# First batch in 512-token blocks with 128-token rows, weight products in tick 2, output copies that scale

## Chip, cores, metric

One core of a Trainium2 chip (trn2) runs the whole program as one launch. The metric is device time in microseconds (us). The kernel before takes 2289.72 us, the median of 3 runs (2289.04 to 2291.06).

## What is computed

x has 4 batches of 12480 tokens with 128 channels. 32 inducing points attend to all tokens of a batch, then every token attends to the 32 results, and a layer with a rational activation follows.

```python
def mab(q, kv):
    s = scale * (q @ kv.transpose(0, 2, 1))
    s = s - s.max(-1, keepdims=True)
    a = np.exp(s)
    a /= a.sum(-1, keepdims=True) + 1e-09
    return a @ kv
h = mab(I, x)                      # 32 rows per batch
x = mab(x, h).reshape(B * S, D)    # 49920 tokens
h = x @ w_in                       # 128 -> 2048
P = a[0] + a[1] * h + a[2] * h2 + a[3] * h3
Q = 1.0 + np.abs(b[0]) * np.abs(h) + np.abs(b[1]) * h2
out = (P / (Q + 1e-6)) @ w_out     # 2048 -> 128
```

The weights arrive as 64-bit words and are turned into 32-bit floats in the kernel (`convert_weights`, line 37: for each word VectorE, DVE in the profile, does six operations and GpSimd, POOL, one add between them).

## The kernel before

All engine calls pass one helper (line 187), so that nearly every row of the profile reads L187, and rows are told apart by their tile names. Within an engine the instructions run in the order in which the program issues them.

**First batch** (`before`, line 1062). `pass1(0)` multiplies the 32 inducing rows with the columns of x (input `x_c`, channels on the partitions): blocks of 480 tokens, four blocks to a group (tile `pc`), 7 groups. DVE copies each group into `e` and keeps a running maximum (`mxs`), from which `nmc` comes. ACT takes the exponentials of `e`. `pooled(0)` turns `e` on TensorE (PE) into `eT` by way of `pt`, 120 tokens to a chunk, and sums the rows of x (input `x_t`, 120 tokens on the partitions) weighted with it, in `ph`; DVE adds each group to `acc`. The fold of `acc` (`pq`), `H` and `HT` end it. Columns and rows of x lie in 9 rooms of the wide tile `row`, 1920 columns wide; a row load has 12 chunks and is issued as two DMAs, of 96 and of 24 partitions (`wide_rows`, line 390). Between these steps the steps of `converted` (line 331) are filled in on DVE; in group 3 DVE also sums `e`.

**Start of the main part** (`main`, line 1120). `pass3(0)` for group 0 makes the token weights `at` of the first four blocks. Pieces 0 and 1 make half of the stationary tile `st` (w_in times `HT`: `pg`, `gs`, `st`). Then ACT scales all of `w_out` by `z_rho`.

**Ticks** (`fast_ticks`, line 953). There are 832 units: 4 batches, 26 blocks of 480 tokens, 8 pairs of slices of the hidden layer. Each tick begins one unit: PE makes `hp` (`first`) and adds a constant to it (`by`, `same`), DVE masks or ACT takes the absolute value into a room of `row`, DVE makes `l`; ACT works on groups of ten units, with logarithm then sigmoid over wide rows of up to 3840 columns; DVE or POOL finishes `l`; 17 ticks behind, PE multiplies `l` with `w_out` into `po` (`second`), of which there is one buffer. After the last pair of a block two more matmuls with `lin` are added, and DVE copies `po` to `oT` (`fetch`, line 938), which goes to `out`.

**Side work** (`side`, line 847). In every tick a budget in us per engine (`SPARE`) lets two generators step on. `attend` (line 825) makes `at` for the blocks to come (tiles `pd`, `sT`, `ps`, `a`, `pa`, `hl`). `ahead` (line 797) first runs `products` and `linear(0)` and then the passes of the batches 1 to 3 (`xTa`, `pc`, `e`). `products` (line 600) makes two sums: `base` times all slices of w_out (32 small matmuls, all in `two`), and w_in, turned by PE into `pgt` and scaled by ACT into `wt`, times w_out, which gives `w_two`. `linear` (line 626) makes `lin` from `w_two` and `HT` (tiles `prep`, `gl`). `attend` isn't stepped before `linear(0)` is done. Where the ticks need what isn't ready, `until` (line 886) steps both generators with no budget until it is: in `second` for `made` (the end of `products`) and for "linear", in `first` for `at`. In this mode nothing of the main loop is issued between.

```python
for which in ("attend", "ahead") if not self.fast or "linear" in self.ready_cols[0] else ("ahead",):
...
if n % 2 == 0 and q == 0:
    self.until(lambda: key in self.at)
```

Of the kernel before, what the change touches and what calls it, by code (L numbers as in the profile page):

```python
# [10 lines left out]
F32 = mybir.dt.float32  # L11
# [6 lines left out]
ALU = mybir.AluOpType  # L18
# [184 lines left out]
class Kernel:  # L203
# [169 lines left out]
    def wide_columns(self, b):  # L373

        def load(g):
            n = min(4, self.NB - 4 * g) * BT
            t = self.room(f"xTw{b}_{g}")
            cuts = [0, BT, 2 * BT, n] if g == 0 and n > 2 * BT else [0, n]
            for lo, hi in zip(cuts, cuts[1:]):
                self.nc.sync.dma_start(out=t[:, lo:hi], in_=self.x_c[b, :, 4 * BT * g + lo:4 * BT * g + hi])  # L380
            return t

        ts = [load(g) for g in range(self.NG)]
        for g, t in enumerate(ts):
            for j in range(4):
                yield t[:, BT * j:BT * j + BT]
                if j == 0 and g > 0:
                    self.wide_rows(b)

    def wide_rows(self, b):  # L390

        xs = self.xs.setdefault(b, [])
        n = min(3 * HB, self.NCH - HB * len(xs))
        if n > 0:
            if len(xs) >= 2 * 3:
                self.words += [w for w in [next(self.loads, None)] if w]
            t = self.room(f"xw{b}_{len(xs)}")[0:TP, 0:n * C].rearrange("p (c d) -> p c d", d=C)
            for p in (slice(0, 96), slice(96, TP)):
                self.nc.sync.dma_start(out=t[p], in_=self.x_t[b, p, HB * len(xs):HB * len(xs) + n, :])
            xs += [t[:, HB * i:HB * i + HB] for i in range(n // HB)]  # L400

    def pass1(self, b):
# [6 lines left out]
        xs = Blocks([], self.wide_columns(b), ahead=False) if self.boot else self.cols.pop((b, "a"))  # L409
# [14 lines left out]
        if self.boot:  # L424
            self.wide_rows(b)
        else:
            self.xs[b] = [self.x_rows(b, n) for n in range(4)]
# [17 lines left out]
        self.e[b] = e  # L445
        self.exps.append(lambda: self.exp_rows(b, e, nmc))
        self.flush()

    def exp_rows(self, b, e, nmc):
# [8 lines left out]
        if g + n < self.NG:  # L458
            if self.boot:
                self.exp_rows(b, e, nmc)  # L460
            else:
                self.exps.append(lambda: self.exp_rows(b, e, nmc))
# [9 lines left out]
    def pooled(self, b, own=None):  # L472
# [17 lines left out]
        eTs, early, n = [], int(self.boot), C if self.boot else C + 1  # L490
# [3 lines left out]
        if early:  # L494
            yield from turned(0)
        for g in range(self.NG):
            nb = min(4, self.NB - 4 * g)
            if g + early < self.NG:
                yield from turned(g + early)
# [3 lines left out]
            for k in range(HB * nb):  # L503
# [5 lines left out]
                if c == 0 and self.boot and (4 * g + j) % 3 == 0 and g + j:  # L509
                    self.xs[b] = xs  # L510
                    self.wide_rows(b)
                nc.tensor.matmul(ph[M * c:M * c + M, 0:n], eT[:, c, M * j:M * j + M], xs[4 * g + j][:, c, :], start=(j == 0), stop=(j == nb - 1))
                if c == HB - 1 and not self.boot and 4 * g + j + 4 < self.NB:
# [7 lines left out]
            if early and g == self.NG // 2:
                full, rest = self.NB // 4, self.NB % 4
                nc.vector.tensor_reduce(out=acc[:, C:], in_=e[:, 0:full].rearrange("p g n -> p (g n)"), axis=mybir.AxisListType.X, op=ALU.add)
                if rest:
                    more, rows = ap.tile([P, 1], F32, tag="mx", name=f"sum{b}"), slice(0, M * rest)
                    nc.vector.tensor_reduce(out=more[rows], in_=e[rows, full], axis=mybir.AxisListType.X, op=ALU.add)
                    nc.vector.tensor_tensor(out=acc[rows, C:], in0=acc[rows, C:], in1=more[rows], op=ALU.add)
# [20 lines left out]
        self.HT[b] = HT  # L548

# [50 lines left out]
    def products(self):  # L600

        nc, ap, p = self.nc, self.ap, self.params
        two = self.ps_o.tile([P, 512], F32, tag="po", name="two")
        for f in range(self.NF):
            if f % 4 == 0:
                yield "pe", 1.0
            nc.tensor.matmul(two[:, C:2 * C], self.base, self.w_out[:, f], start=(f == 0), stop=(f == self.NF - 1))
        yield "v", 0.25
        nc.vector.tensor_scalar(out=self.base, in0=two[:, C:2 * C], scalar1=Z * Z / A16, scalar2=None, op0=ALU.mult)
        for j in range(self.NF // 4):  # L610
            yield "pe", 0.9
# [3 lines left out]
            wt = ap.tile([P, 512], F32, tag="gs", name=f"wt{j}", bufs=2)  # L615
            yield from self.act(lambda: nc.scalar.activation(wt, pt, AF.Identity, bias=0.0, scale=p.lin_scale))
            self.free()
            yield "pe", 1.0
            for i in range(4):
                f = 4 * j + i  # L620
                nc.tensor.matmul(two[:, 0:C], wt[:, P * i:P * i + P], self.w_out[:, f], start=(f == 0), stop=(f == self.NF - 1))
        yield "v", 0.25
        nc.vector.tensor_copy(out=self.w_two, in_=two[:, 0:C])
        self.made = True
# [291 lines left out]
    def second(self, u, ks=(0, 1)):  # L916
# [3 lines left out]
        if q == 0 and 0 in ks:  # L920
            self.until(lambda: self.made or not self.fast)
# [16 lines left out]
    def fetch(self):  # L938
# [5 lines left out]
        self.nc.vector.tensor_copy(out=oT, in_=po[:, 0:BT])  # L944
# [117 lines left out]
    def before(self):  # L1062
# [11 lines left out]
        ahead = self.pass1(0)  # L1074
        next(ahead)
# [7 lines left out]
        self.fill = self.converted(first)  # L1083
        for n, _ in enumerate(ahead):
            for _ in range(4 if n == 0 else 2 if n % 3 == 2 else 0):
                next(self.fill, None)
        self.fill = itertools.chain(self.fill, self.converted(self.words))
# [125 lines left out]
```

## Time and profile before

| what | value |
|---|---|
| median of 3 runs | 2289.72 us |
| the profiled execution: its time, its span | 2289.09 us, 2287.2 us |
| PE, DVE, ACT, POOL busy, share of the span | 94%, 94%, 92%, 65% |
| mean granted TensorE clock | 0.976 |
| DMA | 120.89 MB, mean 53 GB/s |
| chain that ended last | PE 40%, DVE 25%, issue 15%, ACT 14%, DMA 3% |

The busy shares are means over the span. In the 40 slices of 57 us that the page shows, PE, DVE and ACT are at 8 tenths or below in the first four and at 9 in nearly all others, so a stage of the start and the loop have to be read apart. The chain's steps that are named DMA lie in the first 200 us.

### The profile page before, as it was taken

To read this page: it belongs to the slowest core of one execution; us is meant where nothing else is said; L and a number is where in the kernel's file an instruction comes from. 1 tells how busy PE (TensorE), PEld (TensorE's weight loads), DVE (VectorE), ACT (ScalarE), POOL (GpSimd) and SP (SyncE) were. 2 spreads that over 40 slices of the span, in tenths; PEclk is the share of its full clock that TensorE was granted. 3 is DMA by queue.
4 is the path that set the end of the run, shared out by engine and by line. 5 is a ranking of instruction groups with operands and counts; after the bars stand their busy time and mean duration, and the time that the engine had idled before them with its cause. 6 is when DMAs were issued, how large, how long until landed. Compare 5 with 4: busy or idle time off the path is not lost.

```text
span 2287.2 us, 23816 instructions
## 1 busy us (share of the span) xinstructions
PE 2149.3 (94%) x7774; PEld 978.8 (43%) x7774; DVE 2145.6 (94%) x2363; ACT 2101.6 (92%) x1194; POOL 1481.9 (65%) x1030
## 2 busy tenths in 40 slices
PE   4688999999999999998999999989999999999998
PEld 2333444444444444443444444434444444444443
DVE  6786999999999999999999989999999999999995
ACT  1476999999999999998999999989999999999995
POOL 2144666767667666666666666766677776766667
PEclk7799999999999999999999999999999999999999
DMA  9214100220231112212221131001101001000000
GB/s 279 63 57 130 54 13 29 74 79 31 91 96 36 51 35 61 65 48 67 90 60 56 35 91 35 14 23 51 54 16 52 22 17 31 18 22 18 19 12 19
DMA packets 104540, 120.89 MB, mean 53 GB/s; under 512 B 13407, under 2 KB 101279, under 8 KB 104407
## 3 DMA queue, kind: packets, MB, share of 16 engines
q1 hardware_dynamic: 104406, 119.28, 17.5%
q8 instruction: 63, 1.03, 0.2%
q14 instruction: 71, 0.57, 0.1%
HBM read 80.89 MB, written 25.56 MB: 47 GB/s over the span
## 4 chain that ended last, share of the span: by engine, by line
PE 40%; DVE 25%; issue 15%; ACT 14%; DMA 3%; POOL 1%; SPq 1%; ACTq 0%; DVEq 0%; POOLq 0%
PE po L187 26%; DVE l L187 14%; ACT row L187 11%; PE hp L187 10%; DVE row L187 7%; ACT L187 2%; DMA row<-x_t 1%; PE ph L187 1%; PE pc L187 1%; DVE oT L187 1%; SPq L187 1%; POOL l L187 1%; PE pd L187 1%; DVE gl L187 1%; DMA raw<-w_out 1%
## 5 line engine op out<-in xcount | busy, mean ns | idle before, releaser
L187 PE MATMUL po<-l,w_out 128*128 128x480 f32 x3328 | 1555.3, 573 | 5.9 <-POOL l L187 3.3
L187 DVE SCALAR_TENSOR_TENSOR l<-row,all,hp 128x960 f32<-128x960 f32 x832 | 999.5, 1202 | 30.3 <-ACT row L187 24.0
L187 POOL TENSOR_TENSOR l<-row 128x960 f32<-128x960 f32 x416 | 931.4, 2239 | 34.6
L187 POOL TENSOR_SCALAR row<-l,all 128x960 f32<-128x960 f32 x416 | 445.2, 1070 | 672.1 <-DVE l L187 554.5
L187 PEld LDWEIGHTS po<-l,w_out 128*128 128x128 f32 x3328 | 617.6, 191 | 404.2 <-issue 239.9
L187 ACT ACTIVATE row<-row,all 128x3840 f32<-128x3840 f32 (+1 forms) x250 | 738.1, 2953 | 1.0
L187 ACT ACTIVATE row<-row 128x3840 f32<-128x3840 f32 (+1 forms) x250 | 715.8, 2863 | 9.4 <-DVE l L187 8.2
L187 DVE SCALAR_TENSOR_TENSOR l<-l,all,row 128x960 f32<-128x960 f32 x416 | 532.3, 1280 | 2.1 <-ACT row L187 2.1
L187 PE MATMUL hp<-at,st 128*128 128x480 f16 x1664 | 475.6, 368 | 41.5 <-DVE l L187 36.8
L187 ACT ACTIVATE row<-hp,all 128x960 f32<-128x960 f32 x416 | 436.4, 1049 | 51.8 <-PE hp L187 51.3
L187 DVE TENSOR_SCALAR row<-hp 128x960 int32<-128x960 int32 x416 | 475.1, 1142 | 9.3 <-PE hp L187 8.2
L187 PEld LDWEIGHTS <-st 128*128 128x128 f16 x1872 | 181.4, 97 | 523.1 <-issue 502.0
L187 PE MATMUL hp<-same,by 96*128 96x480 f16 x832 | 238.6, 367 | 23.5 <-DVE row L187 22.6
L187 ACT ACT_TABLE_LOAD x169 | 216.8, 1283 | 3.6 <-PEq L1206 0.7
L187 PEld LDWEIGHTS <-by 96*128 96x128 f16 x832 | 82.0, 99 | 215.6 <-issue 194.9
L187 DVE COPY oT<-po 128x480 f32<-128x480 f32 x104 | 67.6, 650 | 41.9 <-PE po L187 41.5
L187 PE MATMUL po<-at,st 128*128 128x480 f16 x208 | 60.5, 373 | 3.2 <-DVE st L187 3.2
L187 POOL TENSOR_TENSOR cv<-cv 128x384 f32<-128x384 f32 (+2 forms) x11 | 12.4, 1126 | 48.6 <-DVE cv L187 48.6
L187 POOL TENSOR_TENSOR a<-a,asm 120x512 f32<-120x512 f32 (+1 forms) x27 | 36.7, 1359 | 6.0 <-DVE asm L187 6.0
L187 DVE TENSOR_SCALAR_CACHE_REDUCE e<-pc 128x240 f32<-128x240 f32 (+1 forms) x56 | 20.5, 399 | 21.1 <-PE pc L187 21.1
L187 ACT ACTIVATE e<-e,nmc 128x960 f32<-128x960 f32 (+1 forms) x16 | 15.5, 986 | 26.4 <-DVE nmc L187 26.4
L187 ACT ACTIVATE hl<-pa 128x480 f16<-128x480 f32 (+1 forms) x28 | 15.6, 558 | 25.1 <-PE pa L187 23.3
(116 smaller groups left out, 610.7 us busy)
## 6 DMA issues: line engine op xcount, KB each, us to landing
xTb<-x_c SPq DMA_DIRECT2D x104, 240.0 KB, 2.8
out<-oT SPq DMA_DIRECT2D x104, 240.0 KB, 2.0
xTa<-x_c SPq DMA_DIRECT2D x78, 240.0 KB, 3.6
x<-x_t SPq DMA_DIRECT2D x78, 240.0 KB, 3.9
at<-hl SPq DMA_DIRECT2D x416, 30.0 KB, 1.8
row<-x_c SPq DMA_DIRECT2D x5, 960.0 KB
row<-x_t SPq DMA_DIRECT2D x8, 576.0 KB, 15.8
raw<-w_in SPq DMA_DIRECT2D x4, 480.0 KB
```

What stands on the lines that cost most here:

```text
L187: ins = call(*args, **kw)
```

## The change

1. `first_batch` takes the place of `pass1(0)` and `pooled(0)`: blocks of 512 tokens and chunks of 128. The columns come in nine tiles of 1536 (the last 192), the rows from a new input `x_r`, in which token 128k+p lies in partition p: one DMA of 128 partitions for each tile, into the room of the column tile that was read last. One load of w_out goes ahead of each row load. More steps of `converted` stand in the score groups: 4 and then 3 for each group.
2. `turned_weights` (the `pgt` turns and ACT's `wt`) stands between the pooled sums, from group 2 on; three `wt` lie in a room of `row`, the fourth in a `gs` buffer.
3. `sums`: POOL adds up the 16 slices of w_out, so that `base` is multiplied once. `products` and `linear(0)` are run whole in ticks 2 and 3, `checks` in tick 4; `ahead` begins with batch 1, `attend` is free from tick 4 on, and `made` with its wait is gone.
4. ACT no longer scales w_out; `fetch` multiplies by `z_rho` as it copies `po`.

```diff
-        xs = Blocks([], self.wide_columns(b), ahead=False) if self.boot else self.cols.pop((b, "a"))
+        xs = self.cols.pop((b, "a"))
...
+    def first_batch(self):
...
+        for lo in range(0, N, 3 * W):
+            cols.append(self.room(f"c{lo}"))
+            nc.sync.dma_start(out=cols[-1][:, 0:min(3 * W, N - lo)], in_=self.x_c[0, :, lo:min(lo + 3 * W, N)])
...
+            t = self.room(f"r{k}")[:, 0:12 * P].rearrange("p (k d) -> p k d", d=C)
+            nc.sync.dma_start(out=t[:, 0:n], in_=self.x_r[:, k:k + n])
...
+        self.some(4)
+        for g in range(groups):
...
+                nc.tensor.matmul(pc[M * j:M * j + M, 0:w], self.ind, cols[i // 3][:, lo:lo + w], start=True, stop=True)
+            self.some(3)
...
+            for _ in range(len(rows), len(cols) if g == groups - 1 else (blocks[-1] + 1) // 3):
+                self.words += [x for x in [next(self.loads, None)] if x]
+                load()
+        nmc = self.filled(self.largest(0, mxs), [1, 1])
...
+        ready = turned(0)
+        turns = self.turned_weights()
+        for g in range(groups):
+            eT, sizes = ready
+            if g + 1 < groups:
+                ready = turned(g + 1)
...
+                    nc.tensor.matmul(ph[M * c:M * c + M, 0:C], eT[0:d, c, M * j:M * j + M], rows[k // 12][0:d, k % 12], start=(j == 0), stop=(i == some[-1]))
+            self.some(5)
...
+            if g > 1:
+                next(turns, None)
...
+    def turned_weights(self):
...
+            lo = 2 * P + 4 * P * j
+            wt = self.row[:, self.rooms["u"] - 1, lo:lo + 4 * P] if j < 3 else self.ap.tile([P, 512], F32, tag="gs", name=f"wt{j}", bufs=2)
+            nc.scalar.activation(wt, pt, AF.Identity, bias=0.0, scale=p.lin_scale)
...
+    def sums(self):
...
+        G.tensor_tensor(out=part, in0=w[:, 0:n], in1=w[:, n:], op=ALU.add)
+        while n > 2 * P:
+            n //= 2
+            G.tensor_tensor(out=part[:, 0:n], in0=part[:, 0:n], in1=part[:, n:2 * n], op=ALU.add)
+        G.tensor_tensor(out=self.w_two, in0=part[:, 0:P], in1=part[:, P:2 * P], op=ALU.add)
...
+            nc.tensor.matmul(two[:, 0:C], wt, self.w_out[:, f], start=(f == 0), stop=(f == self.NF - 1))
+        nc.tensor.matmul(two[:, C:2 * C], self.base, self.w_two, start=True, stop=True)
...
-        if self.fast:
-            yield from self.products()
-            yield from self.linear(0)
...
-            self.until(lambda: self.made or not self.fast)
...
-        self.nc.vector.tensor_copy(out=oT, in_=po[:, 0:BT])
+        if self.fast:
+            self.nc.vector.tensor_scalar(out=oT, in0=po[:, 0:BT], scalar1=self.params.z_rho, scalar2=None, op0=ALU.mult)
...
-            p.checks()
-            nc.scalar.activation(self.w_out, self.w_out, AF.Identity, bias=0.0, scale=p.z_rho)
-        self.later = pieces[2:]
+            self.sums()
+        self.later = pieces[2:] + ([self.products(), self.linear(0), self.checked()] if fast else [])
...
+        "x_r": x[0, :N // P * P].reshape(N // P, P, C).transpose(1, 0, 2),
```

The instructions are moved in these places. `hp_0_2` is the `hp` of block 0, pair 2; the numbers at the end of a name count tiles.

SyncE's (SP's) queue of loads, first batch. Before, from the third load of rows on (`row<-x_t`; `raw` is a load of w_out):

```order
L187 DMA row<-x_t 96x1536
L187 DMA row<-x_t 24x1536
L187 DMA row<-x_t 96x1536
L187 DMA row<-x_t 24x1536
L187 DMA raw_236<-w_out 128x384
L187 DMA row<-x_t 96x1536
L187 DMA row<-x_t 24x1536
L187 DMA raw_250<-w_out 128x384
```

After, from the first load of columns on:

```order
L187 DMA row<-x_c 128x1536 x8
L187 DMA row<-x_c 128x192
L187 DMA raw_213<-w_out 128x384
L187 DMA row<-x_r 128x1536
L187 DMA raw_226<-w_out 128x384
L187 DMA row<-x_r 128x1536
L187 DMA raw_241<-w_out 128x384
L187 DMA row<-x_r 128x1536
```

A tile of rows is now one DMA of 128 partitions instead of two of 96 and 24, a load of w_out stands ahead of each from the first on, and each row load waits for the column tile whose room it takes.

DVE, the products and `linear(0)`. Before, between unit 22 (`l_2_6`) and the mask of unit 24 (`hp_3_0`):

```order
L187 SCALAR_TENSOR_TENSOR l_2_6_970<-row,all,hp_2_6_939 128x960
L187 COPY sT_1_991<-pd_1_978 128x480
L187 SCALAR_TENSOR_TENSOR gl_995<-prep_993,base 128x128
L187 TENSOR_REDUCE amx_1_683<-ps_1_997 120x16
L187 TENSOR_TENSOR a_1_682<-ps_1_997,amx_1_683 120x512
L187 SCALAR_TENSOR_TENSOR gl_995<-gl_995 128x128 x4
L187 SCALAR_TENSOR_TENSOR st_547<-gl_995 64x128 x3
L187 MEMSET st_547 64x64
L187 TENSOR_SCALAR row<-hp_3_0_962 128x960
```

After, between the masks of units 2 and 4 (`hp_0_2`, `hp_0_4`):

```order
L187 TENSOR_SCALAR row<-hp_0_2_677 128x960
L187 SCALAR_TENSOR_TENSOR l_0_1_694<-row,all,hp_0_1_664 128x960
L187 TENSOR_SCALAR base<-two 128x128
L187 COPY w_two<-two 128x128
L187 SCALAR_TENSOR_TENSOR l_0_2_722<-row,all,hp_0_2_677 128x960
L187 SCALAR_TENSOR_TENSOR gl_726<-prep_724,base 128x128
L187 SCALAR_TENSOR_TENSOR gl_726<-gl_726 128x128 x4
L187 SCALAR_TENSOR_TENSOR st_566<-gl_726 64x128 x3
L187 MEMSET st_566 64x64
L187 TENSOR_SCALAR row<-hp_0_4_718 128x960
L187 SCALAR_TENSOR_TENSOR l_0_3_740<-row,all,hp_0_3_690 128x960
```

The whole of `linear(0)`, from `gl` to the memset, stands 20 units earlier, ahead of the mask of unit 4; `sT`, `amx` and `a` of attend's group 1 are no longer beside it.

SP, the DMAs that spread `hl` of group 1 into `at_1_0` (needed by unit 32, `hp_4_0`). Before:

```order
L187 DMA xTa_18_1160<-x_c 128x480
L187 DMA xTa_19_1163<-x_c 128x480
L187 DMA xTa_20_1170<-x_c 128x480
L187 DMA xTa_21_1173<-x_c 128x480
L187 DMA xTa_22_1176<-x_c 128x480
L187 DMA xTa_23_1179<-x_c 128x480
L187 DMA at_1_0_1191<-hl_1_1188 32x480 x8
```

After:

```order
L187 DMA xTa_12_967<-x_c 128x480
L187 DMA xTa_13_970<-x_c 128x480
L187 DMA xTa_14_973<-x_c 128x480
L187 DMA xTa_15_976<-x_c 128x480
L187 DMA out<-oT_0_1056 128x480
L187 DMA at_1_0_1084<-hl_1_1042 32x480 x8
```

Before, the `at` DMAs are queued behind 24 column loads of batch 1 (`xTa`, the last six shown); after, behind 16 and the first output. DVE's last operation ahead of them, `hl_1`, is behind `l_3_1` (unit 25) after, and before it stood between `pc_4` and `pc_5` of batch 1 with only `l_2_0`, `l_3_6` and `pc_5` left to the mask of unit 32.

## Rows read from the trace of the kernel before

**Rows 1.** Windows by stage: window, length, PE PEld DVE ACT POOL busy (x), PEclk, DMA share, GB/s.

```profile
32.40:68.40 36.00, 18.86 (x237) 12.73 (x237) 22.01 (x45) 7.38 (x11) 6.00 (x6) 0.55 0.92 214
...
85.40:102.10 16.70, 12.31 (x68) 7.54 (x69) 13.48 (x14) 9.76 (x13) 5.15 (x6) 1.00 0.08 22
102.10:128.20 26.10, 17.99 (x76) 11.49 (x75) 20.07 (x19) 26.05 (x16) 5.25 (x4) 0.80 0.00 0
...
144.50:153.90 9.40, 4.21 (x20) 1.38 (x20) 6.64 (x15) 5.90 (x3) 0.44 (x1) 0.84 0.63 209
...
171.20:194.30 23.10, 14.16 (x46) 2.82 (x46) 6.96 (x22) 4.35 (x3) 3.03 (x4) 0.87 0.58 176
...
500.00:1400.00 900.00, 876.25 (x3280) 399.48 (x3279) 878.28 (x931) 869.11 (x491) 610.64 (x437) 0.99 0.20 60
```

**Rows 2.** Windows of two stretches of loading: columns, then rows with w_out.

```profile
12.00:24.00 12.00, 8.89 (x39) 0.97 (x36) 7.97 (x29) 0.00 (x0) 2.98 (x4) 0.74 1.01 425
26.00:42.00 16.00, 10.15 (x91) 6.29 (x87) 10.42 (x31) 5.21 (x7) 3.34 (x3) 0.61 1.03 220
```

**Rows 3.** Timeline of PE, 85 to 98 us: start, us, instruction, count, [idle before].

```profile
85.38 0.98 PE L187 MATMUL hp<-at,st 128*128 128x480 f16 x4 [1.91 <-POOL st L187]
...
94.46 1.95 PE L187 MATMUL two<-w_out,base 128*128 128x128 f32 x16
```

**Rows 4.** Timeline of ACT, 84 to 215 us.

```profile
87.63 2.00 ACT L187 ACTIVATE w_out<-w_out,all 128x2048 f32<-128x2048 f32 x1 [2.12 <-DVE w_out L187]
...
100.09 0.68 ACT L187 ACTIVATE wt<-pgt,all 128x512 f32<-128x512 f32 x1
...
102.08 3.40 ACT L187 ACTIVATE row<-row 128x3840 f32<-128x3840 f32 x1
...
128.24 3.40 ACT L187 ACTIVATE row<-row 128x3840 f32<-128x3840 f32 x1
...
210.62 3.40 ACT L187 ACTIVATE row<-row 128x3840 f32<-128x3840 f32 x1
```

**Rows 5.** Timeline of DVE at two copies of the output, blocks 1 and 13.

```profile
198.63 0.66 DVE L187 COPY oT<-po 128x480 f32<-128x480 f32 x1 [1.05 <-PE po L187]
...
446.01 0.65 DVE L187 COPY oT<-po 128x480 f32<-128x480 f32 x1
```

**Rows 6.** Timeline of DVE, 30 to 72 us.

```profile
32.22 0.15 DVE L187 COPY nmc<-pb 128x1 f32<-128x1 f32 x1
...
38.59 0.29 DVE L187 COPY acc<-ph 128x128 f32<-128x128 f32 x1 [3.12 <-PE ph L187]
...
46.26 1.15 DVE L187 TENSOR_SCALAR cv<-raw 128x384 int32<-128x384 int32 x1
47.45 0.56 DVE L187 SCALAR_TENSOR_TENSOR cv<-raw,cv 128x384 int32<-128x384 int32 x1
48.04 0.36 DVE L187 TENSOR_SCALAR cv<-cv 128x384 int32<-128x384 int32 x1
...
55.85 3.14 DVE L187 TENSOR_REDUCE acc<-e 128x1 f32<-128x2880 f32 x1
```

**Rows 7.** Chain of waits, 0 to 150 us: start, us, step.

```profile
22.13 15.98 DMA row<-x_t
```

**Rows 8.** Timeline of DVE, 143 to 156 us.

```profile
149.28 1.26 DVE L187 SCALAR_TENSOR_TENSOR gl<-gl 128x128 bf16<-128x128 f32 x4
```

**Rows 9.** Groups by form: names, shapes xcount | busy us, mean ns | idle before.

```profile
L187 POOL TENSOR_TENSOR l<-row 128x960 f32<-128x960 f32 x416 | 931.4, 2239 | 34.6
...
L187 DVE COPY oT<-po 128x480 f32<-128x480 f32 x104 | 67.6, 650 | 41.9 <-PE po L187 41.5
...
L187 DVE COPY HT<-HT 128x128 f32<-128x128 f32 x4 | 1.1, 281 | 0.2 <-PE HT L187 0.2
```

**Rows 10.** DMA issues, part 6 of the page: out<-in, count, KB each, us to landing.

```profile
at<-hl SPq DMA_DIRECT2D x416, 30.0 KB, 1.8
```

**Rows 11.** The tile gs: ns min/median/max, first and last start, form.

```profile
L187 DVE TENSOR_SCALAR gs<-pg,all x24: 466/500/535, 524.2 to 1486.2; 128x256 f32<-128x256 f32 x24
```

More of the change, by code (lines that the diff above doesn't have):

```diff
@@ L423, in pass1, with largest @@
             self.free()
[L424 to L427, printed above, removed]
+        self.xs[b] = [self.x_rows(b, n) for n in range(4)]
+        nmc = yield from self.largest(b, mxs)
+        self.e[b] = e
+        self.exps.append(lambda: self.exp_rows(b, e, nmc))
+        self.flush()
+    def largest(self, b, mxs):
+        nc, ap = self.nc, self.ap
+        X = mybir.AxisListType.X
         yield "v", 0.1
@@ L458, in exp_rows @@
         if g + n < self.NG:
[L459 to L462, printed above, removed]
+            self.exps.append(lambda: self.exp_rows(b, e, nmc))
     def flush(self):
@@ L508, in pooled @@
                     ph = self.misc(f"ph{b}_{g}")
[L509 to L513, printed above, removed]
+                nc.tensor.matmul(ph[M * c:M * c + M, 0:C + 1], eT[:, c, M * j:M * j + M], xs[4 * g + j][:, c, :], start=(j == 0), stop=(j == nb - 1))
+                if c == HB - 1 and 4 * g + j + 4 < self.NB:
                     xs.append(self.x_rows(b, 4 * g + j + 4))
@@ L516, in pooled, with rows_of @@
             if g == 0:
-                nc.vector.tensor_copy(out=acc[:, 0:n], in_=ph[:, 0:n])
+                nc.vector.tensor_copy(out=acc, in_=ph[:, 0:C + 1])
             else:
-                nc.vector.tensor_tensor(out=acc[:, 0:n], in0=ph[:, 0:n], in1=acc[:, 0:n], op=ALU.add)
+                nc.vector.tensor_tensor(out=acc, in0=ph[:, 0:C + 1], in1=acc, op=ALU.add)
             self.free()
[L521 to L527, printed above, removed]
+        yield from self.rows_of(b, acc)
+    def rows_of(self, b, acc, own=None):
+        nc, ap = self.nc, self.ap
         yield "pe", 0.3
@@ L598, in split @@
         self.ready_cols[b].add(which)
[L600 to L609, printed above, removed]
+    def turned_weights(self):
+        nc, p = self.nc, self.params
+        self.wt = []
         for j in range(self.NF // 4):
-            yield "pe", 0.9
             pt = self.misc(f"pgt{j}")
@@ L1082, in before @@
         nc.vector.memset(self.ceps, CEPS)
[L1083 to L1087, printed above, removed]
-        self.filled(self.pooled(0, self.cp.tile([C, 4 * M], F32, name="HT0")), [5] * self.NG + [2, 2])
+        self.fill = itertools.chain(self.converted(first), self.converted(self.words))
+        self.first_batch()
     def filled(self, gen, most):
         last = None
-        for need, _ in gen:
+        while True:
+            try:
+                need, _ = next(gen)
+            except StopIteration as done:
+                return done.value
             if need == "v" and last == "pe":
-                for _ in range(most.pop(0)):
-                    next(self.fill, None)
+                self.some(most.pop(0))
             last = need
```

142 lines of the change are left out of this document (94 added, 48 removed).

## The prediction

> **What bounds the kernel now.** I read the windows first, stage by stage, because the busy shares of the whole span hide the start. In the loop, from 500 to 1400 us, PE, DVE and ACT are busy 97%, 98% and 97% of the time [rows 1]: there nothing waits, and an edit is worth what it adds to or takes from all three at once. The stages before it look different. From 12 to 24 us the DMA engines are full (1.01) and bring 425 GB/s of columns, while DVE is busy 8.0 of 12 us [rows 2]. From 32.4 to 68.4 they are at 0.92, but move only 214 GB/s, while PE is busy 18.9 us of 36 and DVE 22.0 [rows 1]. From 144.5 to 153.9 and from 171.2 to 194.3 ACT is busy 5.9 of 9.4 and 4.4 of 23.1 us [rows 1]. These two gaps are `until`: side work that the ticks need is made up with the main loop standing still.
>
> Then the timelines, for the borders of the stages. The first `hp` starts at 85.38 [rows 3]. Of ACT's logarithms [rows 4] the first group starts at 102.08, the second at 128.24, and the fourth only at 210.62. Ten units lie between two groups, so that the last step is 82.4 us for twenty units. In undisturbed ticks with side work the output copies of blocks 1 and 13 stand at 198.63 and 446.01 [rows 5]: 247.4 / 12 = 20.6 us for a block of eight units, 25.8 for ten.
>
> The terms below are against the profiled execution, 2289.1 us, which is 0.6 under the median of the three runs; I add the 0.6 at the end.
>
> **(a) Pass 1: +2.0.** Twenty-four steps of the conversion stand ahead of the maximum instead of 17, so 7 more on DVE. At 384 wide a step takes 0.36 or 0.56 us [rows 6], at 480 by the same slope 0.45 to 0.7: 3 to 4 us, and a step behind POOL's add can wait. But DVE has a third of the time free while the columns come [rows 2], and these come no later. Ends: 0 (all hidden) and +4; I take the middle. So `nmc`, at 32.22 before [rows 6], comes at about 34.3.
>
> **(b) Pass 2: -8.6.** It lasts from 32.4 to 68.4 us because the rows are late: the chain stays on one row load for 15.98 us [rows 7]. The two stretches of loading, at equal DMA share [rows 2], show why: columns, 128 partitions a DMA, came at 425 GB/s, rows and w_out, the rows in DMAs of 96 and 24, at 220. After the change a row tile has 128 partitions of 6144 bytes in one DMA, the shape of the new column tiles, so I take 425: rows and w_out are 8.5 MB, 20 us, from the end of the columns (26.4) to about 46.5. Then DVE bounds the pass. The first `acc` comes 6.2 us after `nmc`, as before (38.59 against 32.4) [rows 6]. Behind it DVE has 14 SCALAR_TENSOR_TENSOR at 0.55, 15 TENSOR_SCALAR at 0.36, 7 sums of 0.29, the reduction of `e` at 3.14 x 3072/2880 with 0.5 beside it, and about 4 waits for POOL's add (a `cv` of the same size took 1.15 instead of 0.36, so 0.8 each) [rows 6], less some overlap at the starts: 21.2. In total 27.4 instead of 36.0. PE isn't later: its 18.9 us of now [rows 1] and some 4 for the 16 turns of w_in that come in are 23, all at the granted clock of this stage, 0.55, so mostly at the 1.2 GHz level. Ends: with rows at 220 GB/s as before the last lands at about 65, and (a) and (b) together bring 1.8 instead of 6.6; without any wait for POOL it is 3.2 better.
>
> **(c) From acc to HT: -0.6**, as fewer conversion steps are left to stand between. So (a) to (c) bring the first `hp` from 85.4 to about 78.2.
>
> **(d) Ticks 0 to 7: +4.1.** Here the products begin to cost. PE's product is in tick 2: 17 matmuls of two passes each, at 1.95/16 = 0.122 a pass [rows 3], 4.1 us. Before, 32 passes (3.9 us) lay in the same ticks, but nothing of DVE stood behind them; now the copies of `base` and `w_two` do, ahead of `l_0_2`, and of the 4.1 I take 0.6 as covered by the mask and `l_0_1` ahead: 3.5. Then `gl` with its thirds is ahead of the mask of unit 4: eight operations at 1.26/4 = 0.31 [rows 8] and a memset, 2.6. Gone from here is ACT's scaling of w_out, 2.00 us [rows 4], which held up its first absolute value. 3.5 + 2.6 - 2.0 = 4.1. `sums` on POOL, 1920 elements wide in all, takes 1920/960 x 2.24 [rows 9] = 4.5 us and is hidden: it starts before tick 0, and the product comes some 6 us later. If that cover went, the product would wait for it, which with `gl` operations held by POOL makes the upper end, +8.5; the lower is 0 (all of it beside ACT's work).
>
> **(e) Ticks 7 to 17: -0.5.** ACT is the bound here, 26.05 of 26.1 us busy [rows 1]. Three `wt` at 0.68 [rows 4] leave for pass 2, where ACT is busy 7.4 of 36 [rows 1]; the exponentials of group 1's `a` (some 0.6) come in. DVE then is nearly as full, hence not the whole 1.4.
>
> **(f) Ticks 17 to 37: -29.9.** All three uses of `until` lie here. `made` is gone; "linear" is done in tick 3; attend is free from tick 4 instead of tick 24, so that `hl_1` stands behind unit 25 and its DMAs are issued four ticks, some 10 us, ahead of `hp_4_0`. Each takes 1.8 us to land [rows 10]; only if none of the eight overlapped another (14 us) would they be late. So the 82.4 us become 2 x 25.8 = 51.5, -30.9; less 1.0, since by unit 37 `ahead` has made five of batch 1's score groups, where before it had six, and the loop has that to do later.
>
> **(g) The copies: +3.5.** 104 copies of 0.650 us [rows 9] become TENSOR_SCALAR with a pointer scalar, from PSUM. Before has no such row of 480 wide. The nearest is `gs`, the same operation with one or two pointer scalars at 256 wide: 0.466 at least, 0.500 in the middle, 0.535 at most [rows 11]. A copy of 256 would take 0.281 + 128 x (0.650 - 0.281)/352 = 0.415 [rows 9]. The scalars thus cost 0.05 to 0.12; I take 0.055, the end with one scalar. 104 x 0.055 = 5.7 us of DVE. The loop is full, and `po` has one buffer for which the next block waits, so it isn't hidden; but PE and ACT are equally long, so not all of it counts. Ends: 0 and 5.7.
>
> **Sum:** 2.0 - 8.6 - 0.6 + 4.1 - 0.5 - 29.9 + 3.5 = -30.0; 2289.1 - 30.0 + 0.6 = **2259.7 us**.
>
> **The rivals.** *R1, the gaps' work is paid back in the loop.* In the gaps DVE was busy 6.6 and 7.0 us [rows 1], of which some 8 is side work (the rest is a mask, a copy and three `l`), and the loop has no DVE time to spare. Paid in full it is 2268. Against: the 25.8 for ten units already holds ten ticks' side work. *R2, the rows come no faster.* Lines of 6144 bytes came at 220 GB/s; the pitch between partitions stays long, and that may be the cause and not the 96 + 24. Then 6.6 - 1.8 = 4.8 are lost: 2264. *R3, slower:* a DVE operation on `cv` took 1.15 instead of 0.36 beside POOL [rows 6]. If each scaled copy waits for POOL like that, 104 x 0.8 = 83 us come in: 2339. It decides from (30 + 3.5)/104 = 0.32 us a copy. Against: the 24 `gs` operations read PSUM beside a POOL that is busy two thirds of the loop [rows 1], and the longest took 0.535 [rows 11]. The Trainium skill, "SBUF — State Buffer", section "SBUF: two separate sides", has the port of DVE and POOL locked by certain DVE operations with sources in SBUF; the copy reads PSUM, so by it this doesn't happen, and `gs` agrees. *R4, a gap stays:* if pair 2's `at` lands late, or attend isn't in fact earlier, up to the 23.1 us of the second gap [rows 1] come back: 2282. The order above speaks against it. *R5, the scalar is free:* the copy's time is set by its 480 columns alone. Then (g) is nil: 2256.2. Against: the shortest `gs` is over the line of the copies by 0.05. The Trainium skill, "VectorE: DVE Perf Modes", section "The TRN2 errata — SBUF-src ops pay a fixed extra latency per instruction", speaks for it: an operation from PSUM costs 120 + N cycles at 0.96 GHz, by estimate 625 ns here (the row: 650), with no term for the scalar.
>
> **How the numbers follow.** The forecast gets 0.62, R1 0.12, R2 0.10, R5 0.10, R4 0.03, R3 0.03. The range: 2259.7 less the bounds 2.0 of (a), 3.2 of (b), 4.1 of (d) and 3.5 of (g) is 2247; 2259.7 plus 8 of R1 and 4.4 of (d) is 2272, which takes in R2 with the upper bounds of (a) and (g). R3 and R4 are left out. What a measurement of this kernel can tell from no change is 0.2%, 4.6 us; all cases but R3 end below that: faster 0.96, same 0.01, slower 0.03.
>
> **What would show it.** In the profile after: `nmc` near 34; DMA at or above 400 GB/s while rows load, and the last `acc` near 62; first `hp` near 78; the first logarithm some 21 us behind it; no stretch of ten us with ACT half idle between 80 and 200 us; logarithm groups 26 us apart; `oT` as TENSOR_SCALAR at 0.65 to 0.71. It is wrong if the row loads run at 220 GB/s (R2), if `xTa` and `pc` still stand in the chain ahead of `hp_4_0` (R4), if blocks 2 to 13 take more than 20.6 us each (R1, if by side work; (g), if by `oT`), or if `oT`'s longest is far over its median (R3).

## The result, and the profile after

The changed kernel takes 2258.44 us (median of 4 runs, 2257.45 to 2260.96), beside 2290.27 for the kernel before (4 runs): ratio 0.9863, 95% interval 0.9846 to 0.988. The profiled execution took 2257.45 us with a span of 2255.6, 31.6 less than before.

Windows of the changed kernel, by its own stage borders (columns as in [rows 1]); the last line is the stretch of row loads, which answers to the second of [rows 2]:

```profile
34.60:62.00 27.40, 15.14 (x239) 11.30 (x240) 22.29 (x46) 9.62 (x16) 6.11 (x6) 0.75 0.48 190
78.20:100.50 22.30, 16.56 (x72) 7.80 (x72) 15.36 (x22) 8.73 (x12) 9.60 (x10) 0.76 0.20 60
100.50:125.40 24.90, 17.58 (x65) 5.81 (x62) 24.15 (x32) 24.84 (x14) 5.70 (x5) 0.80 0.39 119
125.40:175.70 50.30, 49.18 (x179) 21.35 (x178) 48.31 (x56) 49.87 (x29) 31.85 (x20) 1.00 0.32 94
...
26.00:42.00 16.00, 6.44 (x59) 4.57 (x59) 10.34 (x33) 4.70 (x7) 2.53 (x3) 0.57 1.02 422
```

The rows came at 422 GB/s instead of 220, and DVE is now busy 22.3 of 27.4 us in pass 2; of the rest it waits 4.2 us for the first `ph` (row at 40.75, below). From 125.4 to 175.7, which answers to the 82.4 us with both gaps, ACT is busy 49.9 of 50.3 us: no gap is left.

DVE's timeline: `nmc`, the first and the last `acc` with the reduction of `e` between, then the copy of `base` and the four operations that split `gl` (they answer to [rows 6] and [rows 8]):

```profile
34.45 0.16 DVE L187 COPY nmc<-pb 128x1 f32<-128x1 f32 x1 [0.54 <-PE pb L187]
...
40.75 0.29 DVE L187 COPY acc<-ph 128x128 f32<-128x128 f32 x1 [4.20 <-PE ph L187]
...
49.08 3.34 DVE L187 TENSOR_REDUCE acc<-e 128x1 f32<-128x3072 f32 x1
...
61.60 0.27 DVE L187 TENSOR_TENSOR acc<-ph,acc 64x128 f32<-64x128 f32 x1
...
89.56 0.29 DVE L187 TENSOR_SCALAR base<-two 128x128 f32<-128x128 f32 x1 [3.62 <-PE two L187]
...
91.41 1.27 DVE L187 SCALAR_TENSOR_TENSOR gl<-gl 128x128 bf16<-128x128 f32 x4
```

PE's and ACT's timelines (they answer to [rows 3] and [rows 4]): first `hp`, the product; piece 3, the last absolute value ahead of the logarithms, and the first, second and fourth group of logarithms.

```profile
78.22 0.98 PE L187 MATMUL hp<-at,st 128*128 128x480 f16 x4 [1.64 <-POOL st L187]
...
85.57 2.84 PE L187 MATMUL two<-w_out,row 128*128 128x128 f32 x24
```

```profile
88.01 0.93 ACT L187 ACTIVATE gs<-pg,all 128x256 f32<-128x256 f32 x2 [3.32 <-POOL st L187]
...
98.14 1.06 ACT L187 ACTIVATE row<-hp,all 128x960 f32<-128x960 f32 x1 [5.23 <-PE hp L187]
...
100.51 3.40 ACT L187 ACTIVATE row<-row 128x3840 f32<-128x3840 f32 x1
...
125.45 3.41 ACT L187 ACTIVATE row<-row 128x3840 f32<-128x3840 f32 x1
...
175.71 1.81 ACT L187 ACTIVATE row<-row 128x1920 f32<-128x1920 f32 x1
```

The output copy (it answers to the row of `oT` in [rows 9]): min, median and max ns.

```profile
L187 DVE TENSOR_SCALAR oT<-po,all x104: 699/711/719, 142.7 to 2249.1; 128x480 f32<-128x480 f32 x104
```

### The profile page after: what moved, and what is told of

It is laid out like the page before. It is cut to its first block, busy times and chain, and to the rows that moved or that the text cites. A ratio compares the mean times of both kernels' runs of the same rounds, so it can differ in the third digit from the quotient of the medians.

```text
span 2255.6 us, 23730 instructions
## 1 busy us (share of the span) xinstructions
PE 2129.1 (94%) x7728; PEld 965.1 (43%) x7728; DVE 2150.4 (95%) x2363; ACT 2101.6 (93%) x1194; POOL 1490.3 (66%) x1034
## 4 chain that ended last, share of the span: by engine, by line
PE 37%; DVE 31%; issue 15%; ACT 14%; POOL 1%; SPq 1%; DMA 1%; DVEq 0%; ACTq 0%; POOLq 0%
PE po L187 24%; DVE l L187 16%; ACT row L187 11%; PE hp L187 9%; DVE row L187 8%; ACT L187 2%; DVE oT L187 1%; PE ph L187 1%; PE pd L187 1%; POOL l L187 1%; DVE cv L187 1%; PE pc L187 1%; SPq L187 1%; DVE asm L187 1%; POOL row L187 0%
## 5 line engine op out<-in xcount | busy, mean ns | idle before, releaser
L187 DVE TENSOR_SCALAR oT<-po,all 128x480 f32<-128x480 f32 x104 | 74.0, 712 | 37.9 <-PE po L187 37.3
L187 POOL TENSOR_TENSOR a<-a,asm 120x512 f32<-120x512 f32 (+1 forms) x27 | 42.9, 1588 | 0.0
L187 ACT ACTIVATE e<-e,nmc 128x960 f32<-128x960 f32 (+3 forms) x16 | 15.4, 979 | 28.6 <-DVE nmc L187 28.6
L187 POOL TENSOR_TENSOR st<-gs,st 64x512 f16<-64x512 f32 x16 | 22.2, 1388 | 15.3 <-ACT st L187 14.2
L187 PE MATMUL pd<-xTb,HT 128*32 128x480 f32 x208 | 29.9, 611 | 1.0 <-DVE hl L187 0.6
```

The source lines that it names most:

```text
L187: ins = call(*args, **kw)
```

## Experiments

Ratios are to the kernel before, run beside each version; the changed kernel's is 0.9863. Blocks are counted from 0 and timed by DVE's copies of the output.

**copy_plain: the copies.** This version leaves the factor z_rho out.

```diff
-            self.nc.vector.tensor_scalar(out=oT, in0=po[:, 0:BT], scalar1=self.params.z_rho, scalar2=None, op0=ALU.mult)
+        self.nc.vector.tensor_copy(out=oT, in_=po[:, 0:BT])
```

> The changed kernel with the output copied as it stands, without the factor z_rho (so the scaling is left out altogether). Its copies should fall back from 0.711 to 0.650 us, 104 x 0.061 = 6.4 us of DVE. Theory (term (g): DVE's time on the copy lies on the path, but not all of it): 3 to 5 us less than the changed kernel, and the loop from the fourth group of logarithms to the end 3 to 5 us shorter. Rival R5 (the scalar is free in the end): less than 1 us. Rival that every microsecond of DVE counts in full: 6.4.

Measured: 2255.68 us, ratio 0.9852 (0.9834 to 0.9869), 2.8 less by the medians. The intervals overlap; the traces agree on the size: from the first copy to the last 2103.8 us instead of 2106.5. So of 6.4 us of DVE some 2.7, four tenths, lie on the path, a little less than the 3 to 5 expected.

**attend_late: the start of attend.**

```diff
-        for which in ("attend", "ahead") if not self.fast or "linear" in self.ready_cols[0] else ("ahead",):
+        for which in ("attend", "ahead") if not self.fast or "linear" in self.ready_cols[0] and self.tick >= 24 else ("ahead",):
```

> The changed kernel with attend held back until tick 24, as it was before; products and linear stay in ticks 2 and 3. Theory (term (f): the second gap comes from attend's late start, as pair 2's weights are needed by unit 32): a stretch of 8 to 20 us with ACT mostly idle comes back ahead of hp_4_0, and the time goes up by 8 to 20 us, though ahead has by then done four score groups more than in the changed kernel. Rival (side work is only moved, it costs the same in the loop): no such stretch, or less than 4 us more.

Measured: 2272.85 us, ratio 0.9926 (0.9905 to 0.9948), 14.4 more. ACT's and PE's timelines ahead of `hp_4_0`, which is the PE row at 172.32:

```profile
157.85 0.62 ACT L187 ACTIVATE a<-a 120x512 f32<-120x512 f32 x1
167.88 0.57 ACT L187 ACTIVATE hl<-pa 128x480 f16<-128x480 f32 x1 [9.41 <-PE pa L187]
...
167.24 0.60 PE L187 MATMUL pa<-ident,a 120*128 120x120 f32 x4 [0.86 <-DVE mt L187]
...
172.32 0.96 PE L187 MATMUL hp<-at,st 128*128 128x480 f16 x2 [2.75 <-DMA at<-hl]
```

ACT idles 9.41 us until `pa`, and PE another 2.75 for the DMAs of `at`. The second gap is attend's late start, and nothing makes up for it: the time is up by all of the 14.4 us that block 1 takes longer.

**before_one_dma, rows_120_8, rows_96_32: how many partitions a DMA has.** The first edits the kernel before, the others the changed one (120 in place of 96 for the second).

```diff
-            for p in (slice(0, 96), slice(96, TP)):
+            for p in (slice(0, TP),):
...
-            nc.sync.dma_start(out=t[:, 0:n], in_=self.x_r[:, k:k + n])
+            for p in (slice(0, 96), slice(96, P)):
+                nc.sync.dma_start(out=t[p, 0:n], in_=self.x_r[p, k:k + n])
```

> The kernel before, with each tile of rows loaded by one DMA of 120 partitions instead of two of 96 and 24. Theory A (the split into 96 and 24 halves the rate): rows and w_out come at over 350 GB/s between 26 and 42 us, pass 2 ends 5 to 8 us earlier, the time falls by 4 to 8 us. Theory B (120 partitions, no multiple of 16, is the cause, not the split): the rate stays near 220 GB/s or falls, the time is the same or a few us longer.

> The changed kernel with each row tile loaded by two DMAs, of 120 and of 8 partitions, from the same input. Theory A (the number of partitions of a DMA sets its rate, 128 spreads over the DMA engines and 120 or 24 does not): the stretch from 26 to 42 us falls from 422 to 220 to 260 GB/s and the last acc comes 3 to 8 us later, 2261 to 2266. Theory B (the layout of x_t with 120 tokens to a column of chunks was the cause): the rate stays above 380 GB/s and the time at 2257 to 2260.

> The changed kernel with each row tile loaded by two DMAs, of 96 and of 32 partitions (120 and 8 gave 214 GB/s from 26 to 42 us, 128 in one 422). Theory A16 (the rate falls where a DMA's partitions are no multiple of 16, the number of DMA engines): above 380 GB/s, last acc within 2 us of the changed kernel's 61.6, the time 2256 to 2261. Theory A128 (only a DMA of all 128 partitions is fast): 200 to 260 GB/s, last acc after 68, 2268 to 2274.

Measured: 2291.48 us, ratio 1.0004 (0.9994 to 1.0014); 2272.29 and 2270.99, one run each. The window of row loads in the three, in this order:

```profile
26.00:42.00 16.00, 10.14 (x88) 6.04 (x85) 10.01 (x29) 5.21 (x7) 3.34 (x3) 0.50 0.99 228
```

```profile
26.00:42.00 16.00, 6.43 (x58) 4.39 (x56) 10.38 (x32) 4.53 (x6) 2.71 (x3) 0.57 0.99 214
```

```profile
26.00:42.00 16.00, 6.45 (x54) 4.42 (x55) 10.43 (x32) 4.53 (x6) 3.31 (x3) 0.63 1.03 234
```

One DMA of 120 partitions is as slow as 96 and 24; so is 120 with 8, from the new layout; and so is 96 with 32, both multiples of 16. Of the five ways tried only the DMA of all 128 was fast. So neither the split alone, nor the layout of x alone, nor a multiple of 16 explains it. A DMA of fewer partitions from the new layout without a split was not tried, nor a split of 128 into halves. The Trainium skill, "DMA: Bandwidth & Descriptors", section "Why a DMA increments its semaphore by 16 and not by 1", gives transfers of 96 and 128 partitions 16 engines, and by its rule 32 as well. By the count of engines alone 96 with 32 would be as fast as 128. The run, at 234 GB/s, shows that this count doesn't set the rate here, and no run here shows what does.

DVE in the last of them shows what slow rows cost: the fourth `acc`, the reduction, the last `acc`.

```profile
58.54 0.29 DVE L187 TENSOR_TENSOR acc<-ph,acc 128x128 f32<-128x128 f32 x1 [6.63 <-PE ph L187]
58.75 3.34 DVE L187 TENSOR_REDUCE acc<-e 128x1 f32<-128x3072 f32 x1
...
71.29 0.28 DVE L187 TENSOR_TENSOR acc<-ph,acc 64x128 f32<-64x128 f32 x1
```

The last `acc` is 9.7 us later than with the change, not 4.8, since 12.8 us of DVE, the reduction and three groups' conversions and sums, come behind the late rows. The first copy of the output is then 9.6 us later and the last 12.8; no run tells where the 3 us in the loop come from.

**Early products in the kernel before, and one tick more or less.**

```diff
-        self.later = pieces[2:]
+        self.later = pieces[2:] + ([self.products(), self.linear(0)] if fast else [])
...
-        if self.fast:
-            yield from self.products()
-            yield from self.linear(0)
```

> The kernel before, with its products and linear(0) run whole in ticks 2 and 3 and attend free from there (part 3 of the change alone, with the turns of w_in and their ACT copies in tick 2, and base times all slices). Theory: both gaps vanish, -29 to -32 us between the second and the fourth group of logarithms, and tick 2 becomes some 10 to 14 us longer (32 passes of base, 32 of wt, 16 turns, four ACT copies in a chain), less the 2 us of wt in the ticks behind: 2270 to 2276. Rival R1 (the gaps' work is paid back in the loop): another 8 us, 2278 or more. Rival that the gaps came from pass 2's late end: they stay, and the time is 2289 or more.

Measured: 2287.57 us, ratio 0.9991 (0.9981 to 1.0001): no gain that can be measured. ACT's timeline: the first `wt` of tick 2, the last absolute value ahead of the logarithms, and the first and fourth group of these.

```profile
96.55 0.69 ACT L187 ACTIVATE wt<-pgt,all 128x512 f32<-128x512 f32 x1 [3.91 <-PE pgt L187]
...
115.60 1.06 ACT L187 ACTIVATE row<-hp,all 128x960 f32<-128x960 f32 x1 [6.66 <-PE hp L187]
...
117.97 3.40 ACT L187 ACTIVATE row<-row 128x3840 f32<-128x3840 f32 x1
...
197.37 3.40 ACT L187 ACTIVATE row<-row 128x3840 f32<-128x3840 f32 x1
```

The gaps are gone: the fourth group is 79.4 us behind the first, before it was 108.5 [rows 4]. The start is later by 15.9 us, and at the fourth group 13.2 us are won. The copies of blocks 3 and 57 tell where they went; first in the kernel before, then in this run:

```profile
240.37 0.64 DVE L187 COPY oT<-po 128x480 f32<-128x480 f32 x1
...
1364.34 0.66 DVE L187 COPY oT<-po 128x480 f32<-128x480 f32 x1 [2.09 <-PE po L187]
```

```profile
225.33 0.66 DVE L187 COPY oT<-po 128x480 f32<-128x480 f32 x1
...
1363.76 0.66 DVE L187 COPY oT<-po 128x480 f32<-128x480 f32 x1 [1.56 <-PE po L187]
```

That is 1124.0 and 1138.4 us: of the 15.0 us won at block 3, 0.6 are left at block 57. The next two runs move the start of the side work by one tick: an empty step behind linear(0) in this kernel (first edit), and the checks put into the tick of linear(0) in the changed one (second).

```diff
-        self.later = pieces[2:] + ([self.products(), self.linear(0)] if fast else [])
+        self.later = pieces[2:] + ([self.products(), self.linear(0), iter(())] if fast else [])
...
-        self.later = pieces[2:] + ([self.products(), self.linear(0), self.checked()] if fast else [])
+        self.later = pieces[2:] + ([self.products(), itertools.chain(self.linear(0), self.checked())] if fast else [])
```

> The run before with early products and linear(0), and one empty step behind linear(0), so that attend and ahead start one tick later: their steps then fall on the same units as in the changed kernel, where the checks fill that tick. The run without the empty step was 13 us ahead of before at the fourth group of logarithms and lost 11 us between the copies of blocks 3 and 57. Theory S (what side work falls on which unit decides how much of the loop is lost, and one tick moves it): it keeps its lead as the changed kernel does, 2275 to 2280, and blocks 3 to 57 take 1124 to 1129 us instead of 1138. Rival R1 (the gaps' side work is paid back in the loop in any case): 2285 to 2289 as without the step. Rival W (the place of the rooms, and so how ACT's wide rows are cut, differs from the changed kernel): 2285 to 2289 too.

> The changed kernel with the checks in tick 3, behind linear(0), instead of a tick of their own, so that attend and ahead start one tick sooner; nothing else differs. Theory S (the units on which side work falls decide): the loop loses about 10 us between blocks 3 and 57, 2265 to 2270. Rivals R1 and W: no change, 2257 to 2260.

Measured: 2283.52 us, ratio 0.9968 (0.9957 to 0.9978), and 2267.32 us, 0.9893 (0.9874 to 0.9912). Blocks 3 and 57 of the changed kernel, and of the changed kernel with the start a tick sooner:

```profile
205.08 0.70 DVE L187 TENSOR_SCALAR oT<-po,all 128x480 f32<-128x480 f32 x1
...
1332.98 0.72 DVE L187 TENSOR_SCALAR oT<-po,all 128x480 f32<-128x480 f32 x1 [0.88 <-PE po L187]
```

```profile
205.25 0.72 DVE L187 TENSOR_SCALAR oT<-po,all 128x480 f32<-128x480 f32 x1
...
1342.92 0.72 DVE L187 TENSOR_SCALAR oT<-po,all 128x480 f32<-128x480 f32 x1 [1.67 <-PE po L187]
```

1127.9 us against 1137.7. Nothing but the tick differs, and it costs 8.9 us by the medians. In these blocks the engines work nearly as long in both (PE 1095 and 1098 us, DVE 1099 and 1104, ACT 1092 in both, the granted clock 1.00), so that for PE and ACT most of the difference is waiting.

For the kernel with early products the step brought 6.2 us in these blocks (1132.2 us), less than the 9 expected at least, and its total missed the 2275 to 2280. Its remaining loss was to be the cut of ACT's wide rows:

```diff
+        self.taken += 2
         self.later = pieces[2:] + ([self.products(), self.linear(0), iter(())] if fast else [])
```

> The run before with early products and one empty step, and the rooms of the loop moved on by two, as the changed kernel has them (its first batch takes 18 rooms, that of before 16, of 9 in a ring), so that ACT's wide rows are cut at the same units as in the changed kernel. Without this, blocks 3 to 57 took 1132.2 us, against 1126.4 in the changed kernel with plain copies and 1138.4 without the empty step. Theory W (besides the units of the side work, the cut of the wide rows decides): 1125 to 1128 us for blocks 3 to 57, the total 5 to 7 us less than without it, 2276 to 2280. Rival (the rest of the loss is the gaps' work paid back, R1, or another part of the change): 1131 to 1134 us, the total unchanged at 2282 to 2285.

Measured: 2273.96 us, ratio 0.9933 (0.9916 to 0.9949), and 1125.7 us for the blocks. Theory W holds. Each of these 54 blocks takes the same time, to 0.03 us, as in copy_plain, the changed kernel with plain copies; so with the gaps gone the loop is the changed kernel's. Against the run without the two rooms 46 of the 54 agree to 0.05 us, and the largest difference, 3.1 of the 6.5 us, is in block 14. There the traces show the reason: ACT's logarithm ahead of `eT`, PE's `ph` that waits for `eT`, and the window of 2 us behind that (columns as in [rows 1]), first without the two rooms:

```profile
430.92 3.40 ACT L187 ACTIVATE row<-row 128x3840 f32<-128x3840 f32 x1
...
434.86 1.95 PE L187 MATMUL ph<-x,eT 120*32 120x129 f32 x32 [2.15 <-ACT eT L187]
...
436.00:438.00 2.00, 2.00 (x18) 1.13 (x11) 2.00 (x3) 2.00 (x1) 1.36 (x5) 0.50 0.17 46
```

Then with them:

```profile
427.71 1.81 ACT L187 ACTIVATE row<-row 128x1920 f32<-128x1920 f32 x1
...
430.06 1.09 PE L187 MATMUL ph<-x,eT 120*32 120x129 f32 x32 [0.55 <-ACT eT L187]
...
432.00:434.00 2.00, 2.00 (x8) 0.94 (x7) 2.00 (x3) 2.00 (x1) 2.00 (x3) 1.00 0.18 46
```

Where the row is cut decides whether a piece of 3840 or of 1920 columns stands ahead of `eT`. With the longer one PE waits 1.6 us more; behind the wait the granted clock is at 0.50, the 1.2 GHz level, and `ph` and the six `po` behind it take 1.5 us more (1.95 and 3.35 instead of 1.09 and 2.68). That is the 3.1. The smaller differences, in blocks 33 and 55 for instance, were not followed in this way.

**products_early: the product and linear(0) ahead of tick 0.** Besides, ACT scales w_out, and the copies are plain.

```diff
+        self.two = self.ps_o.tile([P, 512], F32, tag="po", name="two")
+        for f in range(0, 12, 3):
+            self.part(f, f + 3)
...
+        nc.scalar.activation(w, w, AF.Identity, bias=0.0, scale=self.params.z_rho)
+            nc.tensor.matmul(self.two[:, 0:C], wt, self.w_out[:, f], start=(f == 0), stop=(f == self.NF - 1))
...
+            self.drive(self.products())
         self.drive(pieces[0])
+            self.drive(self.linear(0))
         self.drive(pieces[1])
-        self.later = pieces[2:] + ([self.products(), self.linear(0), self.checked()] if fast else [])
+        self.later = pieces[2:] + ([iter(()), iter(()), self.checked()] if fast else [])
```

> The changed kernel with ACT scaling w_out slice by slice as it is converted (ACT idles there), the product with wt on PE behind the last pooled sum and behind the turns of group 0's scores, base's product and linear(0) ahead of tick 0, and plain copies; the ticks of the products and of linear(0) are left empty, so that side work falls on the same units. Theory (term (d): ticks 2 and 3 hold some 6 us that DVE spends waiting for the product and on gl; term (g): 3 us for the copies): the first logarithm comes 3 to 6 us sooner, the total falls by 6 to 9 us, 2249 to 2253. Rival (ticks 0 to 7 are set by pieces 2 and 3 through ACT and POOL anyway): only the copies' 3 us, 2255 to 2256. Rival (PE at the lower clock makes the product hold up pa or pq): 2256 or more.

Measured: 2250.99 us, ratio 0.9822 (0.9806 to 0.9838), 7.4 under the changed kernel. DVE (last `acc`, the four operations on `gl`), then ACT (first logarithm), then PE (first `hp`), then the window between these two:

```profile
62.48 0.27 DVE L187 TENSOR_TENSOR acc<-ph,acc 64x128 f32<-64x128 f32 x1
...
77.17 2.10 DVE L187 SCALAR_TENSOR_TENSOR gl<-gl 128x128 bf16<-128x128 f32 x4
...
95.20 3.41 ACT L187 ACTIVATE row<-row 128x3840 f32<-128x3840 f32 x1
...
78.86 0.98 PE L187 MATMUL hp<-at,st 128*128 128x480 f16 x4 [0.47 <-POOL st L187]
...
78.86:95.20 16.34, 11.90 (x36) 3.57 (x36) 13.73 (x17) 8.70 (x13) 4.81 (x6) 0.79 0.28 82
```

The first logarithm stands 16.3 us behind the first `hp`, instead of 22.3 in the changed kernel and 16.7 before, and 5.3 us sooner in the execution.

**one_tick_later: this version, one tick later.**

```diff
-        self.later = pieces[2:] + ([iter(()), iter(()), self.checked()] if fast else [])
+        self.later = pieces[2:] + ([iter(()), iter(()), iter(()), self.checked()] if fast else [])
```

> The version with early products and plain copies, with one more empty tick ahead of attend and ahead. Its order of side work from unit 27 on is that of the changed kernel with its start one tick sooner (which cost 9 us), not that of the version without the extra tick. Theory S (the units on which side work falls decide, and whether the start falls on an even or an odd tick sets them): 8 to 11 us slower than without the extra tick, 2259 to 2262. Rival (a sooner start is what costs, for instance by loads that collide with the first ticks): no slower, 2250 to 2252.

Measured: 2259.23 us, ratio 0.9859 (0.9842 to 0.9875), 8.2 more. Block by block the loss is the one that the sooner start had: block 9 is 3.01 us faster there and 2.99 here, block 11 loses 4.21 and 4.19, block 42 2.06 and 2.04. So it isn't the earlier start that costs, nor the later: of the three starts tried, one tick apart, the outer two share one pattern of side work and the middle one has the other. That shows that the order decides; why one order costs 9 us more isn't shown. Blocks 9 to 11 together take the same in the changed kernel and with the sooner start (64.7 and 64.5 us), and the loss builds up in smaller steps from block 22 on.

**sums_on_act: DVE's reduction out of pass 2.** On top of products_early.

```diff
-            nc.scalar.activation(e[0:p, lo:hi], e[0:p, lo:hi], AF.Exp, bias=nmc[0:p], scale=1.0 / math.sqrt(C))
+            nc.scalar.activation(e[0:p, lo:hi], e[0:p, lo:hi], AF.Exp, bias=nmc[0:p], scale=1.0 / math.sqrt(C), accum_out=parts[0:p, k:k + 1])
...
-                nc.vector.tensor_reduce(out=acc[:, C:], in_=e[:, 0:full * W], axis=X, op=ALU.add)
+                nc.vector.tensor_reduce(out=acc[:, C:], in_=parts, axis=X, op=ALU.add)
```

> The version with early products and plain copies, and the sum of the exponentials taken by ACT as it makes them (its accumulator output), so that DVE's reduction of e (3.34 and 0.33 us, with a small add) leaves pass 2. Theory (term (b): once the rows come at 422 GB/s, DVE alone bounds pass 2): the last acc comes 3.0 to 3.8 us earlier than in the version without it, and the total falls by 2.5 to 4 us, 2247 to 2248.5. Rival (PE at the lower clock, or the rows, are right behind DVE): less than 1 us, 2250 to 2251. Rival that the accumulator output costs ACT time: the exponentials get longer and the first acc later, no gain.

Measured: 2247.2 us, ratio 0.9804 (0.979 to 0.9817), the lowest median of all, but its interval overlaps that of products_early. DVE, then ACT:

```profile
34.95 0.16 DVE L187 COPY nmc<-pb 128x1 f32<-128x1 f32 x1 [0.54 <-PE pb L187]
...
41.69 0.29 DVE L187 COPY acc<-ph 128x128 f32<-128x128 f32 x1 [4.63 <-PE ph L187]
...
50.08 0.15 DVE L187 TENSOR_REDUCE acc<-parts 128x1 f32<-128x4 f32 x1
...
58.99 0.27 DVE L187 TENSOR_TENSOR acc<-ph,acc 64x128 f32<-64x128 f32 x1
...
35.21 1.15 ACT L187 ACTIVATE e<-e,nmc 128x1024 f32<-128x1024 f32 x1 [29.19 <-DVE nmc L187]
36.27 0.19 ACT L187 ACTIVATION_READ_ACCUMULATOR e<-e,nmc 128x1 f32 x1
```

From `nmc` to the last `acc` it takes 24.0 us instead of 27.3 in products_early: DVE bounds pass 2. The first copy of the output is 3.3 us earlier too; by the last copy the two profiled executions are even, so the gain in the total isn't shown by them. Reading the accumulator costs ACT 0.19 us a piece, and the first `acc` comes 0.4 later behind `nmc`.

## Why the prediction was right, and where it was not

The forecast was 2259.7 with 2247 to 2272, faster; 2258.44 came. The table sets its steps beside the borders in the two profiled executions. One of them, the last `acc` of before (DVE), is this row:

```profile
68.05 0.28 DVE L187 TENSOR_TENSOR acc<-ph,acc 128x128 f32<-128x128 f32 x1
```

| step | forecast | measured |
|---|---|---|
| (a) to `nmc` | +2.0 | 34.45 - 32.22 = +2.2 |
| (b) `nmc` to last `acc` | -8.6 | 27.15 - 35.83 = -8.7 |
| (c) to first `hp` | -0.6 | 16.62 - 17.33 = -0.7 |
| (d) to first logarithm | +4.1 | 22.29 - 16.70 = +5.6 |
| (e) to second group | -0.5 | 24.94 - 26.16 = -1.2 |
| (f) to fourth group | -30.9 | 50.26 - 82.38 = -32.1 |
| lag of (f) and (g), to the end | +4.5 | 2079.9 - 2076.6 = +3.3 |

- **(a), (b), (c)** hold, and (b) for its reason: the loads' rate doubled, DVE became the bound (sums_on_act). The cause that the prediction leaned to, the split into 96 and 24, is too narrow: any DMA of fewer than 128 partitions that was tried was slow. R2 didn't come, but its price of 4.8 us was too low: with slow rows the changed kernel lost 12.6 and 13.9 us, in one run each. The step that failed there is the assumption that DVE's other work runs beside the late rows.
- **(d)** was mis-sized by 1.5 us, and not in what it added. In products_early, where the product, the operations on `gl` and `sums` are out of these ticks, the stretch takes 16.3 us, so together they cost 6.0; forecast were 3.5 + 2.6 (DVE's wait for the product is 3.62). `sums` wasn't wholly covered: it stands on POOL ahead of piece 2's `st`, for which ACT's `gs` of piece 3 waits 3.32 us (88.01), but that lies within the 6.0. What failed is the 2.0 taken off for ACT's scaling of w_out: with the scaling and the products both gone the stretch is only 0.4 shorter than before. The granted clock in it was 1.00 before [rows 1], 0.76 after and 0.79 in products_early, a difference that the forecast didn't have. Whether this took the rest of the 2.0, or the scaling had been hidden, no run tells apart.
- **(e)** came out 0.7 better, near the 1.4 that three `wt` less and one exponential more make of ACT's time.
- **(f)**: both gaps went, for the forecast reason: with early products both are gone from the kernel before, and with a late attend the second comes back (before_early_linear, attend_late). What the step didn't see is that its rate of 25.8 us for ten units isn't given: it hangs on the tick at which side work starts and on the cut of the wide rows. Had the checks not had a tick of their own, 9 us would have been lost again, and the change would have brought 23 instead of 32. That the start fell on the better tick was luck; nothing in the prediction chose it. The same early products in the kernel before brought 3.0 us in place of the 14 to 20 expected: the start cost 15.9 us instead of 10 to 14, and the loop took 14.4 back. With the tick and the rooms put right (early_tick_rooms) it was 15, by the ratio of 0.9933. The lag behind the gaps was 1.9 us from block 3 to 57 (1125.9 with plain copies, 1124.0 before), of which all but 0.6 came back by the last block; 1.0 was forecast. So R1, that the gaps' work is paid back, fell: at most 0.6 us were, not 8.
- **(g)**: a scaled copy takes 0.711 us, 0.061 more (0.055 forecast), and 2.7 us count where 3.5 were taken. R5 falls: the pointer scalar isn't free. The rule quoted for it from the Trainium skill, "VectorE: DVE Perf Modes", section "The TRN2 errata — SBUF-src ops pay a fixed extra latency per instruction", has no term for the scalar; the trace disagrees, with 0.711 against 0.650. R3 falls too: the longest copy took 0.719.
- **R4** did not come: from 125 to 215 us no wait of PE for `at` is left in the trace.

That the total came within 1.3 us is in part luck too: (d) was 1.5 too low, and (e), (f) and the last row 0.7 to 1.2 too high each.

## What to carry to other kernels

A gap in which one chain of work runs alone is won by starting that chain earlier; but the order that a planner then makes is one of several, and moving its start by one step cost more than a quarter of the gain here, so try the neighbours of the start before trusting a rate. When a load is made faster, look at once at what the waiting engine has left to do (here conversions and a sum): that is the next bound, and the price of the load being slow again. Work that only has to be done once belongs where its engine idles, not in the first ticks of a loop that is full.

## What the runs showed of the hardware

- Row loads of 6144 bytes a partition ran at 422 GB/s with 128 partitions in a DMA, and at 214 to 234 with 120, with 120 and 8, with 96 and 32, and with 96 and 24.
- A pointer scalar on a TENSOR_SCALAR of 480 columns from PSUM cost 0.061 us over a copy (medians of 104 each, 0.711 and 0.650; the shortest, 0.699, is longer than any copy).
- A short wait of PE in the full loop cost as much again behind it: after 2.15 us of waiting in block 14 the granted clock was 0.50 from 436 to 438 us, and a block that lost 1.6 us by the wait lost 3.1 in all; after 0.55 us of waiting it stayed at 1.00.
